# A Fourier token filter plus a GELU-gated MLP on one core: token DFT first, parity folds, twiddles inside constants, gelu out of PSUM

## The chip, the cores and the metric

The kernel runs on one core of one Trainium2 chip. The metric is the device time of one execution in microseconds (us); lower is better. Quoted times are medians, and experiments are compared with the kernel before timed in the same rounds on the same chip. The span of a profile is about 2 us shorter than the time of the same run.

PE is the matmul engine, PEld its weight loads, DVE VectorE, ACT ScalarE, POOL GpSimd, SP the engine that issues most DMAs.

## The reference

The input x is 2048 tokens by 512 features in bf16. It is normalised over the features; the result goes through a filter in the Fourier domain (a real 2-D FFT over tokens and features, times a complex weight table, and back) and, in parallel, through a gated MLP. Both are added to x.

```python
def _A_ref(x, w_r, w_i):                      # x: 1 x 2048 x 512; w_r, w_i: 2048 x 257
    X = rfft2(x.astype(float32)) * (w_r + 1j * w_i)
    return irfft2(X, s=(S, D)).astype(bfloat16)

def _B_ref(x, w_gate, w_up, w_down):          # 512 x 1792, 512 x 1792, 1792 x 512
    g = einsum("bsd,df->bsf", x, w_gate)
    u = einsum("bsd,df->bsf", x, w_up)
    return einsum("bsf,fd->bsd", gelu_tanh(g) * u, w_down)

xn = layernorm(x)
out = x + _A_ref(xn, w_r, w_i) + _B_ref(xn, w_gate, w_up, w_down)
```

## The kernel before

Tokens are laid out as s = 16 p + c: partition p (128) and column block c (16). The order is: layernorm, transposes, a dense feature DFT `dA` of all 16 blocks, then 28 GLU blocks interleaved with 33 "spectral groups" of 8 feature frequencies each (token DFT, twiddle multiplies on VectorE, filter, half of the inverse), and at the end the rest of the inverse on PE alone. A GLU block handles 2 x 512 columns: it copies gate and up results out of PSUM, and spells gelu out as x times the sigmoid of a cubic.

```python
def glu_block(sb, fp):
    # ... (for j in 0, 1: four matmuls into g_ps, four into u_ps)
            if sb == 0 and fp < 3:
                nc.vector.tensor_copy(out=xs[:, j, :], in_=g_ps[:])
            else:
                nc.scalar.copy(out=xs[:, j, :], in_=g_ps[:])
            nc.scalar.copy(out=us[:, j, :], in_=u_ps[:])
    # ... (Square on ScalarE, or on VectorE in the first three)
        nc.vector.tensor_scalar(out=sq[:], in0=sq[:], scalar1=0.044715, scalar2=1.0,
                                op0=ALU.mult, op1=ALU.add)
        nc.vector.tensor_tensor(out=sq[:], in0=sq[:], in1=xs[:], op=ALU.mult)
        nc.scalar.activation(out=sq[:], in_=sq[:], func=AF.Sigmoid, scale=2.0 * GELU_C)
        nc.vector.tensor_tensor(out=xs[:], in0=xs[:], in1=us[:], op=ALU.mult)
        nc.vector.tensor_tensor(out=hT_sb[:, 2 * fp:2 * fp + 2, :], in0=sq[:], in1=xs[:], op=ALU.mult)

def spectral_group(g):                        # 33 of them
    # ... token DFT: 2 matmuls of 256 columns into o1_ps
        nc.vector.tensor_tensor(out=m1[:], in0=o1_ps[:, 0:256], in1=T1c, op=ALU.mult)      # twiddles
        nc.vector.tensor_tensor(out=m2[:, 0:128], in0=o1_ps[:, 128:256], in1=T1s, op=ALU.mult)
        nc.vector.tensor_tensor(out=m2[:, 128:256], in0=o1_ps[:, 0:128], in1=T1ns, op=ALU.mult)
        nc.vector.tensor_tensor(out=O1[:], in0=m1[:], in1=m2[:], op=ALU.add)
    # ... combine (3 matmuls), copy, filter (5 VectorE ops), inverse (2 matmuls), copy

for cp in range(NC):                          # at the end, PE alone
    # ... 4 matmuls of 512 columns: feature inverse
    nc.vector.tensor_tensor(out=y_sb[:], in0=y_ps[:], in1=y1[:, cp, :], op=ALU.add)
```

Of the kernel before, what the change touches and what calls it, by code (L numbers as in the profile page):

```python
# [10 lines left out]
P = 128  # L11
BF16 = mybir.dt.bfloat16
F32 = mybir.dt.float32
ALU = mybir.AluOpType
AF = mybir.ActivationFunctionType

S = 2048
D = 512
NC = 16
KD = 264  # L20
NG = 33
# [3 lines left out]
GELU_C = 0.7978845608028654  # L25


def _const_tables():
    cols = {}
    parts = []  # L30
    off = 0

    def add(name, arr):
        nonlocal off
        arr = np.asarray(arr, dtype=np.float64)
        assert arr.shape[0] == P, (name, arr.shape)
        arr = arr.reshape(P, -1)
        cols[name] = (off, arr.shape[1])
        parts.append(arr)
        off += arr.shape[1]  # L40

    add("ident", np.eye(P))
    d = np.arange(D)[:, None]
    kdc = np.arange(257)[None, :]
    kds = np.arange(1, 256)[None, :]
    FDc = np.cos(2 * np.pi * d * kdc / D)
    FDs = -np.sin(2 * np.pi * d * kds / D)
    FD = np.concatenate([FDc, FDs], axis=1)
    FD = FD.reshape(NE, P, D).transpose(1, 0, 2)
    add("FD", FD.reshape(P, -1))  # L50
    p = np.arange(P)[:, None]
    ka = np.arange(P)[None, :]
    C128 = np.cos(2 * np.pi * p * ka / P)
    S128 = np.sin(2 * np.pi * p * ka / P)
    add("R1", np.concatenate([C128, -S128], axis=1))
    add("R2", np.concatenate([S128, C128], axis=1))
    q = np.arange(P)
    cq = (q // 8)[:, None]
    th = 2 * np.pi * cq * ka / S
    ct, st = np.cos(th), np.sin(th)  # L60
    add("T1c", np.concatenate([ct, ct], axis=1))
    add("T1s", st)
    add("T1ns", -st)
    rv = np.arange(P)
    cr = rv // 8
    tr = rv % 8
    mc = np.arange(P)
    tmm = mc // NC
    kbm = mc % NC
    dmm = (tr[:, None] == tmm[None, :]).astype(np.float64)  # L70
    LC = dmm * np.cos(2 * np.pi * cr[:, None] * kbm[None, :] / NC)
    LS = dmm * np.sin(2 * np.pi * cr[:, None] * kbm[None, :] / NC)
    add("LC", LC)
    add("LS", LS)
    add("LnS", -LS)
    qv = np.arange(P)
    tq = qv // NC
    kbq = qv % NC
    nv = np.arange(P)
    cn = nv // 8  # L80
    tn = nv % 8
    dmi = (tq[:, None] == tn[None, :]).astype(np.float64)
    LCi = dmi * np.cos(2 * np.pi * kbq[:, None] * cn[None, :] / NC)
    LSi = dmi * np.sin(2 * np.pi * kbq[:, None] * cn[None, :] / NC)
    add("RI1", np.concatenate([LCi, LSi], axis=1))
    add("RI2", np.concatenate([-LSi, LCi], axis=1))
    kap = np.arange(P)[:, None]
    cprime = (np.arange(P) // 8)[None, :]
    ph = 2 * np.pi * kap * cprime / S
    cph, sph = np.cos(ph), np.sin(ph)  # L90
    add("T2c", np.concatenate([cph, cph], axis=1))
    add("T2s", sph)
    add("T2ns", -sph)
    kdv = np.arange(2 * P)[:, None]
    dv = np.arange(D)[None, :]
    a = np.where(kdv == 0, 1.0, 2.0)
    iDc = a * np.cos(2 * np.pi * kdv * dv / D) / (S * D)
    iDs = -a * np.sin(2 * np.pi * kdv * dv / D) / (S * D)
    iDc = iDc.reshape(2, P, D).transpose(1, 0, 2)
    iDs = iDs.reshape(2, P, D).transpose(1, 0, 2)  # L100
    add("iDc", iDc.reshape(P, -1))
    add("iDs", iDs.reshape(P, -1))
    pm = np.where(np.arange(D) % 2 == 0, 1.0, -1.0) / (S * D)
    add("PM", np.tile(pm[None, :], (P, 1)))
    allc = np.concatenate(parts, axis=1).astype(np.float32).astype(ml_dtypes.bfloat16)
    ric = np.zeros((NC, P, 4 * P), dtype=np.float64)
    for cpv in range(NC):
        phi = 2 * np.pi * np.arange(P)[:, None] * cpv / S
        Mr = C128 * np.cos(phi) - S128 * np.sin(phi)
        Mi = S128 * np.cos(phi) + C128 * np.sin(phi)  # L110
        ric[cpv] = np.concatenate([Mr, Mi, -Mi, Mr], axis=1)
    ric = ric.astype(np.float32).astype(ml_dtypes.bfloat16)
    return allc, cols, ric
# [3 lines left out]
def kernel(  # L117
# [12 lines left out]

    const_np, ccols, ric_np = _const_tables()
    const_h = nc.inline_tensor(const_np, name="spec_consts")
    ric_h = nc.inline_tensor(ric_np, name="spec_ric")

    def cc(t, name):
        o, w = ccols[name]
        return t[:, o:o + w]
# [9 lines left out]
    pln = tc.alloc_tile_pool(name="pln", bufs=1)  # L147

    x_t = pln.tile([P, NC, D], BF16, name="x_t")
    for cg in range(4):  # L150
        nc.sync.dma_start(out=x_t[:, 4 * cg:4 * cg + 4, :], in_=x_v[:, 4 * cg:4 * cg + 4, :])

    CT = pc.tile([P, const_np.shape[1]], BF16, name="CT")
    csplit = ccols["R1"][0]
    cap = const_h.ap()
    nc.sync.dma_start(out=CT[:, 0:csplit], in_=cap[:, 0:csplit])
    ident = cc(CT, "ident")
    FD = cc(CT, "FD").rearrange("p (e j) -> p e j", e=NE)
    R1 = cc(CT, "R1")
    R2 = cc(CT, "R2")  # L160
    T1c = cc(CT, "T1c")
    T1s = cc(CT, "T1s")
    T1ns = cc(CT, "T1ns")
    L_C = cc(CT, "LC")
    L_S = cc(CT, "LS")
    L_nS = cc(CT, "LnS")
    RI1 = cc(CT, "RI1")
    RI2 = cc(CT, "RI2")
    T2c = cc(CT, "T2c")
    T2s = cc(CT, "T2s")  # L170
    T2ns = cc(CT, "T2ns")
    iDc = cc(CT, "iDc").rearrange("p (w d) -> p w d", w=2)
    iDs = cc(CT, "iDs").rearrange("p (w d) -> p w d", w=2)
    PMc = cc(CT, "PM")

    xnT = pc.tile([P, NE, NC, P], BF16, name="xnT")
    Zs = pc.tile([P, 2, NG, NC, 8], BF16, name="Zs")
    Vs = pc.tile([P, NC, 2, NG, 8], BF16, name="Vs")
    WTd = pc.tile([P, 2, 2, S], BF16, name="WTd", tag="wn2")
# [3 lines left out]
    y1 = pc.tile([P, NC, D], BF16, name="y1")  # L183

    nc.sync.dma_start(out=Wg_sb[:], in_=wg_v)
    nc.sync.dma_start(out=Wu_sb[:], in_=wu_v)
    for part, w_in in enumerate((A_w_r, A_w_i)):
        for w in range(2):
            nc.sync.dma_start_transpose(out=WTd[:, part, w, :], in_=w_in[:, P * w:P * (w + 1)])  # L189
    nc.sync.dma_start(out=CT[:, csplit:], in_=cap[:, csplit:])  # L190
    nc.sync.dma_start(out=Wd_sb[:], in_=wd_v)
    nc.gpsimd.memset(Zs[:, 0, NG - 1, :, 1:8], 0.0)
    nc.gpsimd.memset(Zs[:, 1, 0, :, 0:1], 0.0)
    nc.gpsimd.memset(Zs[:, 1, NG - 1, :, :], 0.0)
    wt32 = pc.tile([P, 2, P], BF16, name="wt32")
    nc.gpsimd.memset(wt32[:], 0.0)
    with nc.allow_non_contiguous_dma(reason="single kd=256 column gather (2x2048 elements)"):
        for part, w_in in enumerate((A_w_r, A_w_i)):
            src = w_in[:, 256:257].rearrange("(kb ka) o -> kb (ka o)", kb=NC)
            nc.sync.dma_start(out=wt32[0:NC, part, :], in_=src)  # L200

    eps_t = pln.tile([P, 1], F32, name="eps_t")
    nc.vector.memset(eps_t[:], 1e-5)
    xn = pln.tile([P, NC, D], BF16, name="xn")
    for cg in range(NC // 4):
        stats = pln.tile([P, 4, nc.vector.BN_STATS_DIM], F32, name="stats", tag=f"stats{cg}")
        mv = pln.tile([P, 4, nc.vector.BN_AGGR_DIM], F32, name="mv", tag=f"mv{cg}")
        rstd = pln.tile([P, 4], F32, name="rstd", tag=f"rstd{cg}")
        nmr = pln.tile([P, 4], F32, name="nmr", tag=f"nmr{cg}")
        for j in range(4):  # L210
            c = 4 * cg + j
            nc.vector.bn_stats(out=stats[:, j, :], in_=x_t[:, c, :])  # L212
            nc.vector.bn_aggr(out=mv[:, j, :], in_=stats[:, j, :])
        nc.scalar.activation(out=rstd[:], in_=mv[:, :, 1], func=AF.Sqrt, bias=eps_t[:], scale=1.0)
        nc.vector.reciprocal(out=rstd[:], in_=rstd[:])
        mr = pln.tile([P, 4], F32, name="mr", tag=f"mr{cg}")
        nc.vector.tensor_tensor(out=mr[:], in0=mv[:, :, 0], in1=rstd[:], op=ALU.mult)
        nc.scalar.activation(out=nmr[:], in_=mr[:], func=AF.Identity, scale=-1.0)
        for j in range(4):
            c = 4 * cg + j  # L220
            nc.scalar.activation(out=xn[:, c, :], in_=x_t[:, c, :], func=AF.Identity,  # L221
                                 bias=nmr[:, j:j + 1], scale=rstd[:, j:j + 1])
        for e in range(NE):
            tp_ps = ps.tile([P, 4, P], BF16, name="tp_ps", tag="B", bufs=1)
            for j in range(4):
                c = 4 * cg + j
                nc.tensor.transpose(tp_ps[:, j, :], xn[:, c, e * P:(e + 1) * P], ident)  # L227
# [206 lines left out]
```

## Time and profile before

| kernel before, profiled run | value |
|---|---|
| time | 244.68 us |
| span of the profile | 243.0 us |
| PE busy | 217.1 us, 89% |
| VectorE busy | 188.7 us, 78% |
| ScalarE busy | 168.1 us, 69% |

The first lines of its profile page: busy time of each engine with its share of the span, then busy tenths in 40 equal slices (PEclk is the granted matmul clock in tenths), then the chain of waits by engine.

```profile
PE 217.1 (89%) x1161; PEld 105.0 (43%) x1161; DVE 188.7 (78%) x603; ACT 168.1 (69%) x306; POOL 0.9 (0%) x8
...
PE   0067799979899999999999999999999998988994
DVE  1963287699999959999974999999759666456784
ACT  2398857456898668989764998987658997635100
PEclk9999999999999999999999999999999999999999
...
PE 59%; SPq 12%; ACT 10%; DMA 10%; DVE 7%; issue 2%; ACTq 0%
```

PE is nearly full from the tenth slice on, while VectorE is full from there to the middle as well. Two stretches by time, each line giving the stretch, its length, the busy time of PE, weight loads, VectorE, ScalarE and GpSimd (with counts), the granted clock and the DMA share:

```profile
60.00:80.00 20.00, 18.81 (x103) 9.15 (x102) 19.78 (x70) 18.18 (x31) 0.00 (x0) 1.00 0.13 18
100.00:120.00 20.00, 19.96 (x113) 9.93 (x112) 19.85 (x73) 18.68 (x33) 0.00 (x0) 1.00 0.12 18
```

From 100 to 120 us PE and VectorE both lack less than 1% of the stretch. I add up the matmuls' start times in the trace. At full clock one matmul takes the next one's place after columns/2.4 ns + 2.5 ns (the Trainium skill, "TensorE: Matmul & The Clock Gate", Back-to-back issue gap, gives that sum for an isolated matmul; these traces agree: groups of four 512-column matmuls start 0.86 us apart). What a start lies later than that is idle time, or half clock where each matmul of a row takes about twice its time. The sums, worked out from the trace:

| from the matmul starts, us | before |
|---|---|
| PE's own work at full clock | 204.9 |
| before the first matmul | 11.8 |
| idle between matmuls | 19.1 |
| lost to half clock and like | 3.6 |
| after the last matmul's start | 3.7 |

(The last matmul's own 0.2 us stands in two rows, so that the sum exceeds 243.0.)

The costly groups of the GLU epilogue (line, engine, operation, output <- input, forms, count, busy us, mean ns of one, then idle time before them and what ended most of it):

```profile
L271 ACT CAST us<-u_ps 128x512 bf16<-128x512 f32 x56 | 33.1, 599 | 7.3 <-PE u_ps L265 6.4
L279 ACT ACTIVATE sq<-sq 128x1024 bf16<-128x1024 bf16 x28 | 30.1, 1076 | 3.9 <-DVE sq L278 3.7
L281 DVE TENSOR_TENSOR hT_sb<-sq,xs 128x1024 bf16<-128x1024 bf16 x28 | 19.2, 686 | 3.7 <-ACT sq L279 3.7
```

ScalarE spends on 1024 elements per partition two pairs of 600 ns casts, a square and a sigmoid; VectorE four passes.

### The profile page before, as it was taken

The numbers are of one execution on the slowest core, as the hardware profiler recorded it, in microseconds if no ns is written. First come the engines' busy times: TensorE is split into PE (matmuls) and PEld (weight loads), VectorE is DVE, ScalarE is ACT, GpSimd is POOL, SyncE is SP. The second block draws the span as 40 slices with busy tenths as digits, with TensorE's granted clock in tenths as the row PEclk, the third lists the DMA queues.
The fourth block names the chain that finished last, engine by engine and source line by source line (L and its number), as shares of the span: only waits on it lengthen the run. The fifth ranks groups of instructions, "written<-read, shape, count | busy, mean of one in ns | idle before, by whom it ended". The sixth has DMA issues, their size and how long they took to land.

```text
span 243.0 us, 3612 instructions
## 1 busy us (share of the span) xinstructions
PE 217.1 (89%) x1161; PEld 105.0 (43%) x1161; DVE 188.7 (78%) x603; ACT 168.1 (69%) x306; POOL 0.9 (0%) x8
## 2 busy tenths in 40 slices
PE   0067799979899999999999999999999998988994
PEld 0034444435444445454444545454444443444441
DVE  1963287699999959999974999999759666456784
ACT  2398857456898668989764998987658997635100
POOL 1000000000000000000000000000000000000000
PEclk9999999999999999999999999999999999999999
DMA  6999994551011121111111111011110000126243
GB/s 212 396 406 220 259 362 50 25 149 24 11 20 22 16 65 40 15 27 18 23 22 59 38 17 24 11 22 15 31 48 18 0 0 4 36 84 182 68 151 129
DMA packets 31810, 20.16 MB, mean 83 GB/s; under 512 B 22064, under 2 KB 30000, under 8 KB 31664
## 3 DMA queue, kind: packets, MB, share of 16 engines
q1 hardware_dynamic: 31792, 19.94, 31.7%
q8 instruction: 9, 0.15, 0.3%
q14 instruction: 9, 0.07, 0.1%
HBM read 13.64 MB, written 2.10 MB: 65 GB/s over the span
## 4 chain that ended last, share of the span: by engine, by line
PE 59%; SPq 12%; ACT 10%; DMA 10%; DVE 7%; issue 2%; ACTq 0%
PE y_ps L287 18%; PE g_ps L262 12%; PE u_ps L265 12%; SPq L189 9%; DMA wt_90<-in_A_w_i_dram 7%; ACT xs L270 3%; DMA ric_t<-spec_ric 3%; ACT us L271 2%; ACT sq L279 2%; PE ov_ps L337 2%; ACT sq L275 2%; SPq L200 2%; PE ov_ps L338 1%; PE y_ps L400 1%; PE y_ps L398 1%
## 5 line engine op out<-in xcount | busy, mean ns | idle before, releaser
L262 PE MATMUL g_ps<-xnT,Wg_sb 128*128 128x512 bf16 x224 | 62.4, 379 | 1.0 <-ACT us L271 0.9
L265 PE MATMUL u_ps<-xnT,Wu_sb 128*128 128x512 bf16 x224 | 61.7, 379 | 0.0
L287 PE MATMUL y_ps<-Wd_sb,hT_sb 128*128 128x512 bf16 x224 | 51.2, 379 | 0.8 <-DVE hT_sb L281 0.6
L271 ACT CAST us<-u_ps 128x512 bf16<-128x512 f32 x56 | 33.1, 599 | 7.3 <-PE u_ps L265 6.4
L270 ACT CAST xs<-g_ps 128x512 bf16<-128x512 f32 x50 | 29.4, 601 | 5.8 <-DVE hT_sb L281 4.3
L279 ACT ACTIVATE sq<-sq 128x1024 bf16<-128x1024 bf16 x28 | 30.1, 1076 | 3.9 <-DVE sq L278 3.7
L287 PEld LDWEIGHTS <-hT_sb 128*128 128x128 bf16 x224 | 21.3, 98 | 26.5 <-DVE hT_sb L281 2.9
L262 PEld LDWEIGHTS <-Wg_sb 128*128 128x128 bf16 x224 | 21.6, 98 | 18.1 <-issue 1.4
L265 PEld LDWEIGHTS <-Wu_sb 128*128 128x128 bf16 x224 | 21.4, 98 | 18.0
L275 ACT ACTIVATE sq<-xs 128x1024 bf16<-128x1024 bf16 x25 | 27.0, 1079 | 0.3
L227 PE MATMUL tp_ps<-CT,xn 128*128 128x128 bf16 x64 | 7.4, 233 | 16.7 <-ACT xn L221 13.1
L281 DVE TENSOR_TENSOR hT_sb<-sq,xs 128x1024 bf16<-128x1024 bf16 x28 | 19.2, 686 | 3.7 <-ACT sq L279 3.7
L280 DVE TENSOR_TENSOR xs<-xs,us 128x1024 bf16<-128x1024 bf16 x28 | 19.2, 686 | 0.3
L278 DVE TENSOR_TENSOR sq<-sq,xs 128x1024 bf16<-128x1024 bf16 x28 | 19.2, 686 | 0.2
L289 ACT CAST y_78<-y_ps 128x512 bf16<-128x512 f32 x16 | 9.2, 585 | 13.9 <-PE y_ps L287 13.9
L240 PE MATMUL dA<-CT,xnT 128*128 128x512 bf16 x64 | 16.6, 402 | 0.2 <-DVE Zs L245 0.2
L276 DVE TENSOR_SCALAR sq<-sq 128x1024 bf16<-128x1024 bf16 x28 | 11.8, 421 | 4.0 <-ACT sq L275 4.0
L326 ACT CAST X2s<-x_ps 128x256 bf16<-128x256 f32 x33 | 12.3, 372 | 3.7 <-PE x_ps L324 3.4
L227 PEld LDWEIGHTS <-xn 128*128 128x128 bf16 x64 | 5.1, 103 | 21.3 <-ACT xn L221 14.3
L339 DVE CAST Vs<-ov_ps 128x256 bf16<-128x256 f32 x33 | 13.8, 419 | 0.0
L291 ACT ACTIVATE nb<-CT,nyq_sb 128x512 bf16<-128x512 bf16 x16 | 11.3, 719 | 3.5 <-DVE y_78 L292 3.5
L212 DVE BATCH_NORM_STATS2 stats<-x_t 128x6 f32<-128x512 bf16 x16 | 10.5, 665 | 4.2 <-DMA x_t<-in_A_x_dram 4.2
(589 smaller groups left out, 313.6 us busy)
## 6 DMA issues: line engine op xcount, KB each, us to landing
x_t<-in_A_x_dram SPq DMA_DIRECT2D x4, 512.0 KB
wtab<-WTd SPq DMA_DIRECT2D x64, 32.0 KB
xr<-in_A_x_dram SPq DMA_DIRECT2D x16, 128.0 KB
ric_t<-spec_ric SPq DMA_DIRECT2D x16, 128.0 KB
out_dram<-y_sb SPq DMA_DIRECT2D x16, 128.0 KB
Wg_sb<-in_B_w_gate_dram SPq DMA_DIRECT2D x1, 1792.0 KB
Wu_sb<-in_B_w_up_dram SPq DMA_DIRECT2D x1, 1792.0 KB
Wd_sb<-in_B_w_down_dram SPq DMA_DIRECT2D x1, 1792.0 KB
```

Source lines behind the costliest of these rows:

```text
L189: nc.sync.dma_start_transpose(out=WTd[:, part, w, :], in_=w_in[:, P * w:P * (w + 1)])
L240: nc.tensor.matmul(dA[:], lhsT=xnT[:, e, c, :], rhs=FD[:, e, :], start=(e == 0), stop=(e == NE - 1))
L262: nc.tensor.matmul(g_ps[:], lhsT=Wg_sb[:, e, fc * P:(fc + 1) * P], rhs=rhs_all[:, e, :], start=(e == 0), stop=(e == NE - 1))
L265: nc.tensor.matmul(u_ps[:], lhsT=Wu_sb[:, e, fc * P:(fc + 1) * P], rhs=rhs_all[:, e, :], start=(e == 0), stop=(e == NE - 1))
L270: nc.scalar.copy(out=xs[:, j, :], in_=g_ps[:])
L271: nc.scalar.copy(out=us[:, j, :], in_=u_ps[:])
L275: nc.scalar.activation(out=sq[:], in_=xs[:], func=AF.Square)
L278: nc.vector.tensor_tensor(out=sq[:], in0=sq[:], in1=xs[:], op=ALU.mult)
L279: nc.scalar.activation(out=sq[:], in_=sq[:], func=AF.Sigmoid, scale=2.0 * GELU_C)
L280: nc.vector.tensor_tensor(out=xs[:], in0=xs[:], in1=us[:], op=ALU.mult)
L281: nc.vector.tensor_tensor(out=hT_sb[:, 2 * fp:2 * fp + 2, :], in0=sq[:], in1=xs[:], op=ALU.mult)
L287: nc.tensor.matmul(y1_ps[:], lhsT=hT_sb[:, f, cl * P:(cl + 1) * P], rhs=Wd_sb[:, f, :], start=(f == 0), stop=(f == NFC - 1))
```

## The change

The intent is to take work away from every engine:

- The token DFT comes first, on normalised rows that are folded by parity (lo + hi, lo - hi), so that the feature DFT works on 128-row quarters: 641 columns in place of 2048 for 128 rows.
- Twiddle factors go into the constant matrices, so VectorE multiplies by none; the 33 groups become 8 larger ones.
- gelu is one ScalarE function that reads PSUM; up times gelu is one VectorE multiply that reads PSUM.
- The last inverse token DFT is one more matmul into the PSUM bank of the down projection.
- The filter's table rows are loaded straight and by indirect DMAs from GpSimd. One row of group 0 holds other frequencies than the rest and is mended by seven small GpSimd operations on one partition ("row fix").
- PSUM copies alternate between ScalarE and VectorE (`evac`).

The diff, cut to its core:

```diff
-            nc.vector.tensor_tensor(out=m1[:], in0=o1_ps[:, 0:256], in1=T1c, op=ALU.mult)
     ... (dA, spectral_group, nyquist_term, x4 and the last inverse go)
+    def pstep(cg, q):                     # token DFT of folded rows, twiddles inside RF
+            nc.tensor.matmul(bp[:, j], lhsT=xf[:, j, q, :], rhs=RF_t[:, 4 * cg + j, :],
+                             start=True, stop=True)
     ...
+    def filt(g):
+        V.tensor_tensor(out=X[:, 0:2], in0=E[:, :, 0], in1=E[:, ::-1, 1], op=ALU.add)
+        V.tensor_tensor(out=X[:, 3:1:-1], in0=E[:, :, 0], in1=E[:, ::-1, 1], op=ALU.subtract)
     ... (copy; m1 = X * tr, m2 = X * ti on 1024 columns; Y, F: four of 512; copy)
+        if g == 0:
+            u = pw.tile([1, 2, 2, 256], BF16, name="u", bufs=1)
+            G = nc.gpsimd
+            E0, F0 = E[0:1], F[0:1]
+            TR0, TI0 = TR[0:1, 0, :, 0:256], TI[0:1, 0, :, 0:256]
+            G.tensor_tensor(out=u[:, 0], in0=E0[:, :, 0], in1=TR0, op=ALU.mult)
+            G.tensor_tensor(out=u[:, 1], in0=E0[:, :, 1], in1=TI0, op=ALU.mult)
+            G.tensor_tensor(out=F0[:, 0], in0=u[:, 0], in1=u[:, 1], op=ALU.add)
     ... (the same for F0[:, 1]; one of 4 columns)
+    def icstep(g):                        # inverse combine: reads F of group g
     ...
+    def glu(sb, fc):
     ... (the eight matmuls into gp and up)
+        nc.scalar.activation(out=ge[:], in_=gp[:], func=AF.Gelu_apprx_tanh)
+        nc.vector.tensor_tensor(out=hT[sb][:, fc, :], in0=up[:], in1=ge[:], op=ALU.mult)
+    def down(c):
     ... (the 14 matmuls of the down projection)
+        nc.tensor.matmul(y_ps[:], lhsT=late["RI"][:, c, :], rhs=late["yt"][:, c, 0:D], start=False, stop=True)
```

All spectral work is spread over the first 41 of 56 GLU units (a unit is now 512 columns); after the 42nd come four rows of the down projection, 14 units, and the other twelve rows.

## The prediction

> **What bounds the kernel now.** Span 243.0 us (time 244.69). Dense matmuls advance 512 columns in 0.216 us (timeline: groups of four start 0.86 us apart). At that rate the listed matmuls sum to: gate and up 448 x 0.216 = 96.8, down 48.4, feature DFT (dA) 13.8, spectral groups 33 x 1536 columns = 21.4, token inverse (x4) 6.9, feature inverse 13.8, transposes 3.5: 205 us. The other 38 us: start (first DFT matmul at 15.7), 3 of tail, waits between. The windows table puts VectorE at 19.8, 19.85 and 19.7 of 20 us from 60, 100 and 140 us, where spectral groups run: there VectorE limits. The chain of waits shows PE 59%, ScalarE 10%, VectorE 7%, and 7% on the 2-byte gather of column 256 (17 us). From 208 us PE runs alone.
>
> **What the change does.**
> - PE: dA, groups, x4 and inverse (55.9 us) become: token DFT 3.5, folded feature DFT 16 x 641 columns 4.3, combine 6.9, inverse combine 6.9, feature inverse 4.3, last inverse 16 x 512 columns 3.5 = 29.4. PE total 178 us, 27 less.
> - ScalarE: per 1024 GLU elements two casts (601 ns each on 512), square (1079) and sigmoid (1076) give way to two gelus out of PSUM. The Trainium skill, "ScalarE: Activation LUTs" (Step-by-step), says every function costs the same per element; square and sigmoid agree. Estimate: 0.60 us per gelu, GLU 34 us instead of 120, ScalarE about 75 in all.
> - VectorE: the four GLU passes become one multiply with a PSUM operand. "VectorE: DVE Perf Modes" (perf-mode tier table) gives two-tensor ops 2x in bf16 SBUF, 1x with PSUM; the trace: 686 ns for 1024 in SBUF, 692 for 512 out of PSUM. Back-to-back ops overlap by about 0.085 us (timeline), so I count 0.60 per multiply, 0.33 per 512-element bf16 op, 0.60 per 512 f32 eviction. Sum: layernorm with Newton rsqrt 22, folds 11, evictions 14, filters 30, unfolds 14, GLU 34, output adds 10 = 135 us (busy 189 before).
> - DMA: WTd transposes, column gather and 64 table copies go; 14 direct loads and 18 indirect ones from GpSimd come. Nothing lands late, I expect.
>
> **Critical path.** From the built order: (1) start: VectorE waits for x[4:8] before it finishes the first layernorm, so gate matmuls start near 13.5 us. (2) The first 42 GLU units carry all spectral work: VectorE about 110 us from there, PE about 100. VectorE limits slightly, and in-order queues with two U buffers lose some 8%: 118 us, to about 132. (3) From there PE alone: four down rows, 14 GLU units, twelve down rows = 13 + 24.2 + 38.9 = 76. (4) Tail 3.3. Span 211, time **212 us**. Range 203 to 223. Faster by over 2%: 0.96; within: 0.03; slower: 0.01.
>
> **What would show it.** First gate matmul at 12 to 15 us; VectorE above 90% busy up to about 130 us and near 30% after; PE waits there mostly on the multiply (u buffers); PE unbroken after the last unfold, for about 76 us; ScalarE near 75 us; one gelu near 600 ns; filter group near 3.7 us of VectorE.
>
> **What would make it wrong.** Folds with reversed rows running at 1x (adds up to 8 us to VectorE); dependent neighbouring VectorE ops costing their full latency (adds 10); indirect loads or GpSimd's table fix later than about 58 us, when the first filter needs them (stalls the in-order VectorE queue); better overlap than 92%, which would give 203.

## More of the kernel before

The kernel before took 244.68, 245.1, 245.19 and 244.9 us in the four sessions.

PE's own work is 84% of the span, and from 30 to 200 us PE idles only about 7.4 us in all.

## The result

The changed kernel took 210.88 us (209.78 to 211.05, four runs) against 244.68 for the kernel before. The ratio is 0.860, with a 95% interval of 0.857 to 0.863. Ratios here are the mean time of one kernel's runs over that of the other's of the same rounds, so they are not quite the ratio of the quoted medians. The same page lines of the changed kernel:

```profile
PE 187.7 (90%) x1040; PEld 94.3 (45%) x1040; DVE 140.3 (67%) x360; ACT 71.5 (34%) x118; POOL 30.3 (15%) x41
...
PE   0079999999999199999999999999999999999992
DVE  2998999999779979999995999323433312212121
ACT  2042434653663335665635775002333300000000
POOL 3777761000043800000000000000000000000000
PEclk9999999999999759999999999999999999999998
...
PE 74%; DVE 13%; POOL 3%; DMA 3%; issue 2%; ACT 2%; SPq 1%; POOLq 0%; DVEq 0%
```

ScalarE is at less than half its former busy time. After the start PE is nearly full everywhere but in the fourteenth slice, in which GpSimd works; the matmul clock falls to 7 tenths there and to 5 in the slice after it. PE's waits (waited for, us in total, times, longest us) and the stretches around it:

```profile
PE tp L285 <- DVE xn L275: 10.6, 1, 10.6
PE gp L422 <- POOL F L407: 4.8, 1, 4.8
PE g_ps L469 <- ACT xnT L289: 1.1, 1, 1.1
PE gp L422 <- DVE F L393: 0.4, 1, 0.4
```

The first of these is the start of the kernel. The second, 4.8 us, has no counterpart before.

```profile
45.00:60.00 15.00, 15.00 (x109) 8.39 (x108) 12.58 (x24) 8.35 (x15) 1.22 (x1) 1.00 0.10 36
60.00:75.00 15.00, 10.14 (x55) 5.27 (x53) 14.81 (x28) 5.71 (x10) 7.49 (x7) 0.86 0.01 2
75.00:90.00 15.00, 15.00 (x86) 7.92 (x85) 13.22 (x33) 8.09 (x14) 0.00 (x0) 0.91 0.00 0
90.00:105.00 15.00, 14.55 (x86) 7.93 (x85) 14.90 (x38) 9.35 (x16) 0.00 (x0) 1.00 0.00 1
105.00:120.00 15.00, 14.98 (x101) 8.38 (x100) 12.79 (x38) 8.77 (x16) 0.00 (x0) 1.00 0.01 2
120.00:135.00 15.00, 15.00 (x92) 7.81 (x90) 11.85 (x43) 6.69 (x12) 0.00 (x0) 1.00 0.03 10
135.00:165.00 30.00, 30.00 (x141) 13.58 (x139) 10.85 (x16) 7.76 (x13) 0.00 (x0) 1.00 0.10 31
```

The columns are those of the stretches before: PE, loads, VectorE, ScalarE, GpSimd, clock. PE is full in almost every stretch; only 60 to 75 us shows 10.14 of 15, with the clock at 0.86. VectorE is near full in some stretches and at 11.9 to 13.2 of 15 in others, while PE goes on in both. From 135 us on PE runs without a gap and VectorE has little to do.

The costly groups that answer to those of before:

```profile
L475 ACT ACTIVATE ge<-g_ps 128x512 bf16<-128x512 f32 x56 | 33.5, 598 | 55.0 <-PE g_ps L469 54.6
L476 DVE TENSOR_TENSOR hT_633<-u_ps,ge 128x512 bf16<-128x512 f32 x14 | 9.5, 682 | 2.2 <-PE u_ps L472 2.2
L422 PE MATMUL gp<-CT,F 128*128 128x256 bf16 x64 | 9.2, 290 | 5.3 <-POOL F L407 4.8
```

One gelu out of PSUM took 598 ns, as long as one of the former casts (599), and one multiply with a PSUM operand 680 to 692 ns. This is what the two places of the Trainium skill that the prediction cites had said.

The same sums of matmul starts for both kernels:

| from the matmul starts, us | before | after | difference |
|---|---|---|---|
| PE's own work at full clock | 204.9 | 178.4 | -26.5 |
| before the first matmul | 11.8 | 10.6 | -1.2 |
| idle between matmuls | 19.1 | 9.1 | -10.0 |
| lost to half clock and like | 3.6 | 6.8 | +3.2 |
| after the last matmul's start | 3.7 | 4.2 | +0.5 |

Of the 34 us, PE's own work is 26.5. Of the 9.1 us idle, 5.0 is the one wait for GpSimd. Of the half clock, 3.5 us fall in the start (10 to 20 us) and 2.5 in the 5 us after that wait. How it comes about, from the timeline of the changed kernel (start, duration, engine, line, operation; in brackets the idle time before and what ended it). L403 to L407 are the row fix, L377 to L392 VectorE's filter of the next groups:

```profile
66.12 1.52 POOL L403 TENSOR_TENSOR F<-u 1x512 bf16<-1x512 bf16 x1 [4.79 <-DVE F L393]
66.67 1.01 DVE L379 COPY X<-E 128x4 bf16<-128x4 bf16 x1
67.72 1.64 POOL L404 TENSOR_TENSOR u<-E,TR 1x512 bf16<-1x512 bf16 x1
68.32 1.59 DVE L386 TENSOR_TENSOR m_818<-X,TI 128x1024 bf16<-128x1024 bf16 x1
69.33 1.53 POOL L405 TENSOR_TENSOR u<-E,TI 1x512 bf16<-1x512 bf16 x1
69.83 0.68 DVE L476 TENSOR_TENSOR hT_633<-u_ps,ge 128x512 bf16<-128x512 f32 x1
70.44 0.71 DVE L388 TENSOR_TENSOR Y<-m_817,m_818 128x512 bf16<-128x512 bf16 x1
70.94 1.21 POOL L406 TENSOR_TENSOR F<-u 1x512 bf16<-1x512 bf16 x1
71.07 1.37 DVE L389 TENSOR_TENSOR Y<-m_817,m_818 128x512 bf16<-128x512 bf16 x1
72.23 0.28 POOL L407 TENSOR_TENSOR F<-E,t_653 1x4 bf16<-1x4 bf16 x1
72.56 1.89 PE L422 MATMUL gp<-CT,F 128*128 128x256 bf16 x8 [4.84 <-POOL F L407]
...
74.78 1.91 PE L469 MATMUL g_ps<-xnT,Wg_sb 128*128 128x512 bf16 x4
```

The row fix is seven operations on one partition, 1.2 to 1.6 us each, the last 0.28. Two have run at 58.8 to 61.3 us; the other five begin when VectorE's own part of group 0 is done, and the inverse combine of group 0 (L422) stands next in PE's in-order queue. And the two engines hold each other up: the copy of 4 columns at 66.67 took 1.01 us (0.16 elsewhere), m2 at 68.32 took 1.59 (0.68 elsewhere), the Y at 71.07 took 1.37 (0.41). Their ends fit a lock that changes hands: the copy ends 0.04 us after the GpSimd operation that began before it; m2 ends 0.55 us after L404 does; Y 0.29 after L406. The multiply at 69.83, which has one operand in PSUM, took 0.68 as always beside L405. The Trainium skill, "SBUF — State Buffer" (Who interferes with whom), says that GpSimd's only SBUF ports are VectorE's second pair, that an instruction holds it exclusively while the other engine blocks, that a VectorE instruction with two SBUF inputs contends with a GpSimd instruction that reads SBUF, and that one with at most one SBUF input outside certain fast modes doesn't contend. The trace agrees in these numbers. The first gate group afterwards (74.78) took 1.91 us for four matmuls in place of 1.03: half clock. The same skill's page on TensorE (Part 1: The HAM clock gate) gives half rate after an idle window of about 3.4 us, until about as long a time of work has passed; the 4.8 us gap and the 2.5 us lost after it agree (the clock that the trace records is at half for 6.8 us from 70.8 us on; in the second trace of this kernel, c0_after, for 3.4 us behind the same gap).

### The profile page after: what moved, and what is told of

The parts are those of the page before. It is cut to its first block, busy times and chain, and to the rows that moved or that the text cites. A ratio compares the mean times of both kernels' runs of the same rounds, so it can differ in the third digit from the quotient of the medians.

```text
span 208.9 us, 2903 instructions
## 1 busy us (share of the span) xinstructions
PE 187.7 (90%) x1040; PEld 94.3 (45%) x1040; DVE 140.3 (67%) x360; ACT 71.5 (34%) x118; POOL 30.3 (15%) x41
## 4 chain that ended last, share of the span: by engine, by line
PE 74%; DVE 13%; POOL 3%; DMA 3%; issue 2%; ACT 2%; SPq 1%; POOLq 0%; DVEq 0%
PE y_ps L482 23%; PE g_ps L469 19%; PE u_ps L472 18%; PE gp L422 3%; DMA x_t<-in_A_x_dram 3%; PE yp L439 2%; PE tp L285 2%; PE dp L336 2%; PE bp L316 2%; PE y_ps L484 2%; DVE hT_177 L476 2%; DVE stats L271 1%; DVE xn L275 1%; ACT xnT L289 1%; DVE hT_1133 L476 1%
## 5 line engine op out<-in xcount | busy, mean ns | idle before, releaser
L475 ACT ACTIVATE ge<-g_ps 128x512 bf16<-128x512 f32 x56 | 33.5, 598 | 55.0 <-PE g_ps L469 54.6
L487 DVE TENSOR_TENSOR y_sb<-y_ps,y_sb 128x512 bf16<-128x512 f32 x16 | 11.1, 691 | 39.2 <-PE y_ps L484 39.2
L476 DVE TENSOR_TENSOR hT_1677<-u_ps,ge 128x512 bf16<-128x512 f32 x14 | 9.7, 692 | 14.6 <-PE u_ps L472 14.6
L285 PE MATMUL tp<-CT,xn 128*128 128x128 bf16 x64 | 6.3, 242 | 10.8 <-DVE xn L275 10.6
L422 PE MATMUL gp<-CT,F 128*128 128x256 bf16 x64 | 9.2, 290 | 5.3 <-POOL F L407 4.8
L354 ACT CAST E<-ep 128x512 bf16<-128x512 f32 x16 | 10.7, 735 | 8.7 <-PE ep L353 5.4
L271 DVE BATCH_NORM_STATS2 stats<-x_t 128x6 f32<-128x512 bf16 x16 | 10.6, 674 | 3.8 <-DMA x_t<-in_A_x_dram 3.7
L482 PE MATMUL y_ps<-Wd_sb,hT_177 128*128 128x512 bf16 x56 | 12.7, 379 | 0.0
L482 PE MATMUL y_ps<-Wd_sb,hT_633 128*128 128x512 bf16 x56 | 12.7, 379 | 0.0
L482 PE MATMUL y_ps<-Wd_sb,hT_1133 128*128 128x512 bf16 x56 | 12.7, 379 | 0.0
L482 PE MATMUL y_ps<-Wd_sb,hT_1677 128*128 128x512 bf16 x56 | 12.7, 379 | 0.0
L476 DVE TENSOR_TENSOR hT_633<-u_ps,ge 128x512 bf16<-128x512 f32 x14 | 9.5, 682 | 2.2 <-PE u_ps L472 2.2
L285 PEld LDWEIGHTS <-xn 128*128 128x128 bf16 x64 | 4.6, 108 | 13.0 <-DVE xn L275 12.6
L422 PEld LDWEIGHTS <-F 128*128 128x128 bf16 x64 | 6.3, 103 | 8.6 <-POOL F L407 5.3
L476 DVE TENSOR_TENSOR hT_177<-u_ps,ge 128x512 bf16<-128x512 f32 x14 | 9.5, 680 | 0.6 <-PE u_ps L472 0.6
L445 ACT CAST yf<-yp 128x512 bf16<-128x512 f32 x16 | 8.5, 591 | 4.1 <-PE yp L439 2.9
L476 DVE TENSOR_TENSOR hT_1133<-u_ps,ge 128x512 bf16<-128x512 f32 x14 | 9.5, 680 | 0.0
L236 POOL DMA_INDIRECT TR<-in_A_w_r_dram,idx_t x9 | 8.7, 971 | 5.0 <-DMA idx_t<-spec_rows 2.6
```

The source lines that it names most:

```text
L236: nc.gpsimd.indirect_dma_start(out=T[:, g, s, 0:W], out_offset=None, in_=w_in[:, :], in_offset=bass.IndirectOffsetOnAxis(ap=idx_t[:, g, s: ...
L271: nc.vector.bn_stats(out=stats[:, j, :], in_=x_t[:, c0 + j, :])
L285: nc.tensor.transpose(tp[:, e, j, :], xn[:, c0 + j, e * P:(e + 1) * P], ident)
L354: nc.scalar.copy(out=E[:, r].rearrange("p s (k t) -> p t s k", t=2), in_=ep[:].rearrange("p (t s k) -> p t s k", t=2, s=2))
L422: nc.tensor.matmul(gp[:, s], lhsT=F[:, s, r, t::2], rhs=cc(f"M{r + 1}" + z), start=(s == 0 and r == 0), stop=(s == 1 and r == 1), skip_gro ...
L445: nc.scalar.copy(out=yf[:, c % 2], in_=yp[:].rearrange("p (t k) -> p t k", t=2))
```

## Experiments

Eleven kernels ran, all giving results that passed the comparison with the reference. Since some of them differ at the start of the kernel, I also compare one stage that no start can touch: from the first up-projection matmul of the eleventh GLU unit to the first matmul of the first down row. It holds nearly all spectral groups; PE's own work in it is 81.6 us. Each value is from one profile; the two of the changed kernel differ by 0.8 us. (In f3_rowfix_warm and f4_all the record of that up-projection matmul is missing; its start is taken 0.2 us before the unit's gelu, as it is in the other traces.)

| kernel | chip | time, us | ratio to before | that stage, us |
|---|---|---|---|---|
| changed, first runs | - | 210.88 | 0.860 | 91.9 |
| e1_evict_act | 7 | 221.61 | 0.906 | 90.1 |
| e2_no_rowfix | 7 | 216.28 | 0.881 | 85.3 |
| e3_rowfix_vec | 7 | 216.20 | 0.881 | 85.1 |
| e4_late_g0 | 7 | 222.76 | 0.908 | 91.9 |
| c0_after (changed, again) | 11 | 210.71 | 0.860 | 91.1 |
| e5_warm | 11 | 209.82 | 0.855 | 91.6 |
| e6_before_gelu | 11 | 241.65 | 0.989 | - |
| e7_after_oldglu | 11 | 233.31 | 0.950 | 105.6 |
| f1_rowfix_vec (same as e3) | 14 | 203.76 | 0.834 | 85.1 |
| f3_rowfix_warm | 14 | 203.68 | 0.834 | 84.8 |
| f4_all | 14 | 203.68 | 0.834 | 84.4 |

### Less work for VectorE: e1_evict_act

```diff
     def evac(o, i):
-        flip[0] ^= 1
-        if flip[0]:
-            nc.scalar.copy(out=o, in_=i)
-        else:
-            nc.vector.tensor_copy(out=o, in_=i)
+        nc.scalar.copy(out=o, in_=i)
```

> The changed kernel with all 48 alternating PSUM evictions on ScalarE (24 leave VectorE, 24 x 0.60 = 14 us of its work; correct result). The prediction on record (VectorE limits the stretch from 13.8 to 129 us): 8 us or more faster, about 202. Rival, from the ledger of matmul starts (PE limits, 101 us of its own work plus 5.0 us for GpSimd's row fix, 6 us at half clock, 3 us of small waits): at most 2 us faster, 209 to 211; the 5 us wait before the first inverse combine stays, VectorE's busy time falls to about 126 us and that of ScalarE rises to about 86.

It took 221.61 us, 11 more than the changed kernel. All four kernels run on chip 7 share that loss, and it lies between 10 and 30 us (see c0_after below). In the stage beyond it, VectorE's busy time fell from 85.1 to 75.2 us, and the stage shortened from 91.9 to 90.1. Ten microseconds less work on VectorE bought two at most (one against c0_after's 91.1), and 1.0 of them came out of the wait for GpSimd itself (3.8 us in place of 4.8). VectorE therefore doesn't set the pace of the stage. f4_all repeats this without the start's loss.

### The row fix away: e2_no_rowfix

```diff
-        if g == 0:
-            u = pw.tile([1, 2, 2, 256], BF16, name="u", bufs=1)
     ... (all seven operations go)
         f_tiles[g] = F
```

One row of group 0 is then wrong; the result still lay within the tolerance of the comparison, so that the comparison can't vouch for that row.

> The changed kernel without the seven GpSimd operations that correct row 0 of filter group 0 (wrong result on purpose). Theory A (PE limits, the row fix holds it): 5.0 us of wait and about 2.5 us of half clock behind it go, 7.5 us faster, about 203.4, and no dip of the granted clock near 70 us. Rival (VectorE limits, so PE would have waited elsewhere): 0 to 3 us faster, 208 to 211.

The time was 216.28 us with the loss common to chip 7; the stage took 85.3 us, 6.6 less than in the changed kernel and 3.7 above PE's own work. The row fix costs about that much (5.8 us against c0_after), over three times what removing 10 us of VectorE work brought in e1.

### The row fix on VectorE: e3_rowfix_vec

```diff
-            G = nc.gpsimd
+            G = nc.vector
```

> The row fix on VectorE in place of GpSimd (correct result): seven operations on one partition, about 2.5 us more VectorE work. Theory A (GpSimd's slowness is the cause): 5 to 7.5 us faster, 203.5 to 206. Rival (VectorE limits): the same or up to 2.5 us slower than now, 210 to 213.

216.20 us with the loss common to chip 7, stage 85.1 us: the same as without any row fix, though VectorE has six operations of about 0.4 us and a small one more. So it is not the work of the fix that cost the time but its place on GpSimd, which is both slow and in VectorE's way.

### The wait moved, not removed: e4_late_g0

```diff
-        F = pw.tile([P, 2, 2, 256], BF16, name="F", bufs=3)
+        F = (pc.tile([P, 2, 2, 256], BF16, name="F0", tag="xn") if g == 0
+             else pw.tile([P, 2, 2, 256], BF16, name="F", bufs=3))
     ...
-        if g == 0:
+        if "G" not in late:
             late["G"] = pc.tile([P, 4, NC, 2, NG, 8], BF16, name="Gs", tag="x_t")
     ...
-            tasks.append(lambda g=g: icstep(g - 3))
+            tasks.append(lambda g=g: icstep((1, 2, 0, 3, 4, 5, 6, 7)[g - 3]))
```

The inverse combine of group 0 comes after those of groups 1 and 2, which gives the GpSimd fix time to finish.

> The row fix stays on GpSimd, but the inverse combine of group 0 is issued after that of groups 1 and 2, so PE does not reach it before GpSimd has ended (correct result). Theory A1 (it is PE's in-order wait for GpSimd that costs): 5 to 7.5 us faster, as without the fix. Theory A2 (it is the stretching of VectorE operations beside GpSimd, the second product 1.59 us in place of 0.68): only 0 to 3 us faster, PE then waits for VectorE's filter of group 1 instead.

222.76 us, stage 91.9 us: nothing gained. PE's waits of this kernel:

```profile
PE gp L423 <- DVE F L394: 3.7, 2, 3.2
PE u_ps L473 <- DVE hT L477: 2.0, 1, 2.0
```

No wait for GpSimd is left, but PE now waits 3.7 us for VectorE's filter of the other groups, and 2.0 us (at 80 to 82 us) for a GLU multiply that stood behind it in VectorE's queue. Both ran beside the row fix; its second product took 1.58 us here too. Of the two theories A2 holds. To hide the latency of the GpSimd operations was not enough, since they cost VectorE's time as well.

### The changed kernel again, as control: c0_after

> The changed kernel, unchanged, as a control. The four runs before this one showed 11 to 12 us of PE idle between 10 and 30 us that the first profile of the changed kernel does not have (1.7 us there), with PE's completion signals arriving late and in a burst near 30 us, although no instruction of that stretch was changed in three of them. Theory C1 (it belongs to the chip or the session, not to the edits): this control shows it too where it runs on the same chip, about 220 us, and the edits of the row fix then count as 4 us faster. Theory C2 (the edits cause it): the control gives 211 us and PE idle of about 2 us there.

210.71 us on another chip, as at first. The 10 to 12 us that e1 to e4 lost between 10 and 30 us are thus either theirs or those of their chip and session. f1_rowfix_vec decided it for e3: its unchanged kernel took 203.76 us on a third chip and shows no such loss. For e1, e2 and e4 it is taken to be the same; they did not run again. What the loss looks like is seen in ScalarE's first copy out of PSUM, which waits for the transposes. First in e3_rowfix_vec (chip 7), then in c0_after:

```profile
19.29 1.01 ACT L289 COPY xnT<-tp 128x1024 bf16<-128x1024 bf16 x1 [17.28 <-remote]
```

```profile
13.75 1.01 ACT L289 COPY xnT<-tp 128x1024 bf16<-128x1024 bf16 x1 [11.74 <-PE tp L285]
```

In e3 the second set of transposes ended at 14.35 us in the trace, but the semaphore signal that tells others so is recorded at 19.27, and ScalarE started on it at 19.29. The first gate matmuls ended at 22.22 us, and their gelu started at 27.95. In c0_after signals follow a matmul's end by 0.01 to 0.02 us, and the first gelu the gate matmuls by 0.03. The recorded signals of e3 can't be read one by one: the next ones stand in a burst at 30.8 to 31.0 us, later than that gelu, and some are missing (22 of VectorE's 305 in the whole trace). What is sure is that the waiting engines started 5 to 6 us late. The kernel before was not slowed on chip 7 (245.1 us). Why they started late there is open, and chip and session are not told apart: the DMA queues are full in that stretch in all runs of the changed kernel, and GpSimd issues its indirect loads then, but the same holds where nothing was late.

### Warming PE up: e5_warm

```diff
+    wz = pc.tile([P, 512], BF16, name="wz", tag="hT1")
+    nc.vector.memset(wz[:], 0.0)
+    wp = ps.tile([P, 512], F32, name="wp", tag="S", bufs=4)
+    for k in range(24):
+        nc.tensor.matmul(wp[:], lhsT=wz[:, 0:P], rhs=wz[:], start=True, stop=True)
     layernorm(0)
```

> The changed kernel with 24 matmuls of zeros from about 1.5 us, before the first real one, so that PE's clock is up when the gate matmuls start (correct result). The first profile has 3.5 us of half-clock loss between 10 and 20 us. Theory W (that loss is on the critical path, PE limits): 2 to 3.5 us faster than the control of this call. Rival (the start is set by the layernorm and the loads, VectorE limits after it): within 1 us of the control.

209.82 us, ratio 0.855 (0.851 to 0.858) against 0.860 (0.858 to 0.863) for c0_after: 0.9 us, with touching intervals. The matmuls ended at 8.5 us, 2.5 us before the first transpose (the expectation of f3_rowfix_warm below says 3.4, a slip), and the first gate matmuls still ran at half clock. The question stayed open until f3_rowfix_warm.

### The gelu part alone: e6_before_gelu

The kernel before, with nothing but its GLU epilogue replaced:

```diff
-            if sb == 0 and fp < 3:
-                nc.vector.tensor_copy(out=xs[:, j, :], in_=g_ps[:])
     ... (copies, square, four VectorE passes, sigmoid go)
+            ge = pw.tile([P, 512], BF16, name="ge", bufs=3)
+            nc.scalar.activation(out=ge[:], in_=g_ps[:], func=AF.Gelu_apprx_tanh)
+            nc.vector.tensor_tensor(out=hT_sb[:, fc, :], in0=u_ps[:], in1=ge[:], op=ALU.mult)
```

> The kernel before with the gelu out of PSUM and one multiply alone; its spectral part stays (correct result). ScalarE's busy time falls by about 86 us and VectorE's by about 35. Ledger theory (PE limits both kernels: 205 us of its own matmuls, 12 us to the first, 19 us of waits, 4 of tail): only waits can go, 4 to 8 us faster, 237 to 241. Rival (ScalarE and VectorE set the pace before, and the gelu is most of the gain): 15 us or more faster, below 230.

241.65 us, ratio 0.989 (0.982 to 0.997): 3.5 us by the medians, 2.8 by the means, which is under the 4 to 8 us that the ledger theory expected and far from the rival's 15. Its busy line:

```profile
PE 215.9 (90%) x1161; PEld 105.1 (44%) x1161; DVE 158.2 (66%) x538; ACT 97.3 (41%) x203; POOL 0.9 (0%) x8
```

ScalarE lost 71 us of work and VectorE 31, and the time hardly moved, because PE's own 204.9 us stayed; PE's idle time went from 19.1 to 16.5 us. In the kernel before, a VectorE at 99% was no limit.

### The rest alone: e7_after_oldglu

The changed kernel with the old epilogue, on 512 columns at a time (`xf` single-buffered to make room):

```diff
-        nc.scalar.activation(out=ge[:], in_=gp[:], func=AF.Gelu_apprx_tanh)
-        nc.vector.tensor_tensor(out=hT[sb][:, fc, :], in0=up[:], in1=ge[:], op=ALU.mult)
+        nc.scalar.copy(out=xs[:], in_=gp[:])
+        nc.scalar.copy(out=us[:], in_=up[:])
+        nc.scalar.activation(out=sq[:], in_=xs[:], func=AF.Square)
     ... (three VectorE passes, sigmoid, last multiply)
```

> The changed kernel with the old epilogue of the GLU (two casts, square and sigmoid on ScalarE, four passes on VectorE, on 512 elements at a time, one fold buffer fewer to make room; correct result). In the 42 units up to the first down row ScalarE then has about 42 x 2.2 + 34 = 126 us and VectorE about 103 + 25 = 128, against 101 of PE. Interaction theory: 15 to 30 us slower than the control, the gelu is what lets the smaller PE work show. Additive theory (the gelu is worth here what it is worth alone): 4 to 8 us slower.

233.31 us, ratio 0.950: 11.9 us less than before, though PE's own work is the 178.4 us of the changed kernel. The busy line, and two of PE's waits:

```profile
PE 195.4 (84%) x1040; PEld 94.9 (41%) x1040; DVE 179.0 (77%) x528; ACT 155.0 (67%) x286; POOL 30.0 (13%) x41
```

```profile
PE u_ps L472 <- ACT us L476: 9.0, 10, 2.2
PE g_ps L469 <- ACT xs L475: 3.2, 7, 0.6
```

PE now waits for ScalarE to empty its PSUM banks; it idles 30.9 us in all. The two parts bring 3.5 and 11.9 us alone, and 34.5 together. Shorter matmul work is worth its length only if the epilogue keeps up, and a shorter epilogue nothing while the matmul work fills the span.

### The row fix on VectorE, on an undisturbed chip: f1_rowfix_vec

The edit is that of e3_rowfix_vec.

> The row fix on VectorE again, the same kernel as e3, because e3 ran on a chip where all four kernels lost 11 us at the start. There the stretch from the eleventh GLU unit to the first down row took 85.1 us against 91.1 to 91.9 in the two traces of the changed kernel. Chip theory (the start stall is of that chip or session): here PE idles about 2 us between 10 and 30 us and the time is 203.5 to 205.5, 6 us below the 210.7 of the control, ratio to the kernel before about 0.834. Edit theory (moving the fix moves the start): about 216 again. If this lands on the first chip, the stall should be there again.

203.76 us (203.71 to 204.82), ratio 0.834 (0.831 to 0.836) against 0.860 for the control: 6.7 us by the means. It differs from the changed kernel in one word, and is faster than both kernels. Its granted clock and PE's waits:

```profile
PEclk9999999999999999999999999999999999999999
```

```profile
PE gp L422 <- DVE F L393: 0.6, 1, 0.6
PE gp L422 <- DVE F L407: 0.5, 1, 0.5
```

The dip of the clock is gone, and what PE waits for the row fix (L407) is 0.5 us in place of 4.8. Some 20 of the matmul records are missing in this trace and in each of the next two, so I give no sums of their matmul starts.

### The last half clock at the start: f3_rowfix_warm

f1_rowfix_vec with the warm-up of e5_warm, 36 matmuls in place of 24, so that they end at about 11.4 us.

> f1 with 36 warm-up matmuls of zeros. With 24 (e5) they ended at 8.5 us, 3.4 us before the first transpose, and the gate matmuls were at half clock all the same (2.5 us lost). With 36 they should end near 11 us. Theory W: the gate matmuls start at full clock, 2 to 3 us faster than f1. Rival: the clock falls again, or the transposes are held back, within 1 us of f1.

203.68 us, the same. The warm-up did what it was meant to: the up matmuls below take 1.03 us for four from the start. But then PE waits:

```profile
14.44 1.03 PE L472 MATMUL u_ps<-xnT,Wu_sb 128*128 128x512 bf16 x4
...
20.47 0.23 PE L285 MATMUL tp<-CT,xn 128*128 128x128 bf16 x1 [1.59 <-DVE xn L275]
```

The last line's bracket says that PE idled 1.59 us until VectorE's second layernorm. The eleventh unit was reached at 35.9 us in place of 36.6 (and at 36.9 in f4_all, which is warmed up as well). Most of the 2 us at half clock were slack: the start is paced by the loads and VectorE's layernorms. Here, up to about 20 us, VectorE does set the pace.

### All three together: f4_all

f3_rowfix_warm with `evac` on ScalarE alone, as in e1_evict_act.

> f3 with all alternating evictions on ScalarE (VectorE 14 us less). Ledger theory (PE limits, VectorE does not): within 1.5 us of f3. The step of the prediction on record (VectorE limits up to the first down row) would have 6 us or more here, now that GpSimd is out of the way.

203.68 us, the same again. From 30 to 120 us, f1_rowfix_vec and then f4_all:

```profile
30.00:120.00 90.00, 88.12 (x581) 49.08 (x590) 85.67 (x227) 53.03 (x91) 3.13 (x8) 1.00 0.12 37
```

```profile
30.00:120.00 90.00, 88.13 (x583) 49.66 (x593) 76.57 (x210) 64.35 (x115) 3.27 (x8) 1.00 0.12 37
```

VectorE went from 85.67 to 76.57 us busy and ScalarE from 53.03 to 64.35, with PE at 88.1 in both. Neither is the limit; PE's own work is what is left.

## Why the prediction was right, and where its reasons were not

The predicted 212 us was met by 210.88, and so were most of its parts. For the middle stage, where its mechanism failed, that is luck:

| part | predicted | measured |
|---|---|---|
| first gate matmul at | 13.5 us | 13.8 |
| from there to the first down row | 118 us | 115.1 |
| from there to the last matmul, PE alone | 76 us | 76.0 |
| one gelu | 0.60 us | 0.598 |
| ScalarE in all | 75 us | 71.5 |
| VectorE in all | 135 us | 140.3 |
| PE's own work | 178 us | 178.4 |

- **The start.** The wait for x[4:8] that the prediction names is in the traces of c0_after (1.01 us) and f1 (0.68), but not in the first one, where VectorE only does that group's statistics in between; the 13.5 us fit either way.
- **PE's work and the last stage.** Right. The 76.0 us after 129 us hold 352 matmuls of 512 columns: 216 ns each, with no gap.
- **The GLU epilogue.** Right in size; ScalarE fell by 97 us.
- **Folds.** The doubt about reversed rows was unfounded: folds took 411 to 416 ns for 512 elements, as straight ones.
- **A slip.** The text counts "two casts (601 ns each on 512)" per 1024 elements. There are four; its sum of 120 us was made with four.
- **The middle stage.** Here the mechanism failed. The step as it stood: "VectorE about 110 us from there, PE about 100. VectorE limits slightly, and in-order queues with two U buffers lose some 8%: 118 us". The stage took 115.1 us, of which PE's own work is 101.5. But VectorE doesn't limit it: about 10 us less VectorE work shortened the counted stage by less than 2 us (e1) or 1 us (f4_all against f1 and f3). PE limits the stage from the eleventh unit on, and the 13.6 us of loss are not spread by queues: 5.0 are the one wait for GpSimd and 2.5 the half clock after it, about 3 the units before the eleventh (2.9 of half clock, of which f3 shows that most is slack behind the loads and layernorms), and the rest small gaps. That the 8% allowance had nearly the right size, for another cause, is luck: without the row fix on GpSimd the same prediction would have been 8 us too high.
- **The term that was missing.** GpSimd's row fix was not in the sum at all. It was counted nowhere among VectorE's or PE's costs; the prediction mentions only GpSimd's *table* fix, as a risk of late data, and that fix was in time. Nor was the time in which it holds VectorE up: VectorE was busy 140.3 us, and 135.3 in e2 without the fix, where the prediction has 135. With the row fix on VectorE the kernel takes 203.76 us, close to the 203 that the prediction named for "better overlap than 92%".
- **What bounds the kernel before.** The prediction read "there VectorE limits" from a VectorE at 19.8 of 20 us. e6 took 31 us of work from VectorE and gained 3.5: the reading was wrong, and the gaps between matmuls would have shown it beforehand.
- **What would show it.** "VectorE above 90% busy up to about 130 us" was not met (12.6 of 15 us and the like), and PE's waits were not "mostly on the multiply": none of PE's waits of 0.4 us or more was.

What remains open is why engines that waited for PE started late on chip 7 in e1 to e4.

## What to carry to other kernels

When two engines are both nearly full, a busy share doesn't tell which of them limits: subtract the matmuls' own time from the distances of their starts, and look at what ends the few gaps that are left. Price the small operations too, above all those that stand alone on a slow engine before a matmul in an in-order queue; seven of them on one partition cost here as much as a fifth of the whole change's gain, and next to nothing on VectorE (PE waited 0.5 us for them). Shortening matmuls and shortening the epilogue that empties their banks belong together: apart they gave 15.4 us, together 34.5.

## What the Trainium skill lacked or had wrong

- "TensorE: Matmul & The Clock Gate" (Back-to-back issue gap) gives, in that section, about 131 ns per 512-column matmul as the sustained rate with weight loads and calls columns/2.4 + 2.5 ns the isolated gap. Here 352 such matmuls, each with its weight load, took 76.0 us without a gap, 216 ns each: the isolated figure is the sustained one.
- "SBUF — State Buffer" (Who interferes with whom) has the lock between VectorE and GpSimd, and the trace agrees; it has no case of operations on a single partition that hold up operations on 128. Here VectorE operations rose from 0.16 to 1.01, 0.41 to 1.37 and 0.68 to 1.59 us beside GpSimd operations of 512 elements on one partition, and moving these to VectorE brought 6.7 us (means of f1_rowfix_vec and c0_after).
- "GPSIMD Engine Reference" (4.1 Engine selection) puts two-input elementwise work at about twice VectorE's time. Here operations of 512 elements on one partition took 1.21 to 1.64 us on GpSimd, part of it blocked, and 0.40 to 0.41 on VectorE: three to four times.
- "ScalarE: Activation LUTs" (Step-by-step) gives one rate per element for every function, and gelu agrees (598 ns); a copy of the same 512 elements that wrote every second element took 735 ns against 591 for one written in a row.
- No page was found to have engines that start 5 to 6 us after the matmuls they wait for have ended (14.35 to 19.29 us and 22.22 to 27.95 us in e3_rowfix_vec on one chip), where 0.03 to 0.04 us is usual.
